# First stage of a routed-attention kernel: low words as unsigned integers on ScalarE, a written order of vector work, deeper loads, later stores

## The chip, the cores and the metric

The kernel runs on one core of a Trainium2 chip. The metric is the device time of one execution in microseconds (us). The engines are TensorE (PE, matrix products; PEld is its weight load), VectorE (DVE), ScalarE (ACT), GpSimd (POOL) and SyncE (SP), which here only issues DMA transfers.

## The reference

Three steps, each feeding the next. Attention packs K and V of 8 batches, 8 heads, 576 tokens into 32 rows per head and reads them back with the queries; a dense layer follows, `g = h - tanh(h)`, and then a layer of 8 experts of which each token takes two.

```
p_packed = sm_attn(p, k, v)                 # 32 rows per head
out      = sm_attn(q, p_packed, p_packed)   # 576 rows per head
x = transpose(out).reshape(4608, 512)
h = x @ w_in;  x = (h - tanh(h)) @ w_out    # 512 -> 2048 -> 512
...                                         # two experts of eight for each row
out[mask] += top2_w[mask, k, None] * (relu(x[mask] @ w1[e]) @ w2[e])
```

The weights `w_in` and `w_out` come as 8-byte floats, which the kernel brings to 4 bytes itself.

## The kernel before

There are three stages, one after the other in the program: `phase_a`, `phase_b`, `PhaseC`.

**First stage, `phase_a`.** It has 16 units, one for each batch and half of the heads. A unit loads keys and packing rows (`load_k`, tile `kT`, 608 KB) and values (`load_v`, 576 KB). Then `s1` multiplies (PE, tile `s`), `max1` takes the negated row maximum (DVE, lines 180 and 181, tile `nm`), `exp1` the exponentials (ACT, line 187, tile `a`), `t1` transposes them (PE, line 199, tile `tp`), `a1t` copies them out (ACT, `a1T`), `pv` multiplies by the values (PE, line 211), `recip1` (DVE, 192 and 193) and `pz2` (DVE, 216, tile `Pz`) scale and mask, `pt` transposes (PE, 221), `pt_out` copies out (ACT, `PT`) and `pt_store` stores 64 KB to memory.

Between the units' steps lies the widening of 28 pieces of `w_in` and `w_out`, class `Widen`. A piece is 128x512 8-byte numbers (512 KB, tile `cvr`). Its high words go through ACT (`act1`, line 69), then DVE (lines 73, 75, 76), its low words through DVE (line 78, which makes a float of the bits) and ACT (`act2`, line 84, which waits for line 78); DVE then makes the scale (line 80) and joins both (`dve2`, lines 88 and 91). That is seven DVE and two ACT instructions for each piece. Four more pieces go the same way in the second stage (tiles `cvc_b`, `cvf_b`, raw tile `wor`).

The loop runs 18 steps. A step handles two pieces (14 steps have them), the scores of unit n and the rest of unit n-1. The string `ORDER` says in what sequence the steps are written, and PE, SP and ACT keep that sequence; DVE's instructions are put in order by the scheduler. SP issues loads and stores from one queue in that order: a store that waits for `PT` holds the loads behind it. Keys and values have two buffers each, raw pieces three.

In steps 3 to 8 the loop also runs the first query chunk (`Queries`, lines 278 to 335): its scores `sq`, two transpositions, a maximum, exponentials, a sum, a transposition to tile `a`. The tiles `q` (the queries as loaded) and `a` share one buffer. `Queries.split` makes `a2h` (ACT) and `a2l` (DVE, line 101) of `a`; it is written at the start of the second stage.

**Second stage, `phase_b`.** It first multiplies `u` (PE, 442, psum tiles of two buffers), splits it into `uh` (ACT, 447) and `ul` (DVE, 451), and then runs 256 steps of `g1` (PE, `h`), `gate` (ACT tanh `t`, DVE `g`), `gsplit` (`gh`, `gl`) and `g2` (PE, `acc`). Around them, a table of steps (`at`) places the widening of the last four pieces, the splits `woh`/`wol`, and constants (`consts_b`) in its first steps. Here PE, ACT, DVE and SP keep the written order.

Of the kernel before, what the change touches and what calls it, by code (L numbers as in the profile page):

```python
# [50 lines left out]
class Widen:  # L51
# [15 lines left out]
    def act1(self):  # L67
        self.c = self.tile("c", F32)
        self.K.nc.scalar.activation(self.c, self.hi.bitcast(F32), AF.Abs)

    def dve(self):
# [6 lines left out]
        V.tensor_scalar(self.f, self.lo, 9, 0x3F800000, op0=ALU.logical_shift_right, op1=ALU.bitwise_or)  # L78
# [25 lines left out]
ORDER = """t1 a1t s1 p0 lk p1 max1 p2 p4 pl r4 rec pv pz2 p3 exp1 pt r0 pto pts qs r1 lv qm qx r2 r3 qa rl""".split()  # L104
ENG = {mybir.EngineType.PE, mybir.EngineType.SP, mybir.EngineType.Activation}
NWA = 12


def phase_a(K, kT, v, w_in, w_out, wide_in, wide_out):
# [4 lines left out]
    with ExitStack() as ctx:  # L114
        right = ctx.enter_context(ExitStack())
        ld = right.enter_context(tc.tile_pool(name="a_ld", bufs=2, side="right"))
# [17 lines left out]
        def cv_load(i):  # L134
            if i < 16:
# [6 lines left out]
            if wide:  # L142
                raw = cv.tile([P, 2 * CW], I32, tag="cv_raw", name=f"cvr_{i}")
# [88 lines left out]
        def on(n, *fs):  # L232
            if 0 <= n < 16:
# [13 lines left out]
        cv_load(1)
        load_v(0)
        for n in range(18):
            c0, c1 = 2 * n, 2 * n + 1  # L250
            ops = {
                "s1": lambda: on(n, s1), "max1": lambda: on(n, max1), "exp1": lambda: on(n, exp1),
                "t1": lambda: on(n - 1, t1), "a1t": lambda: on(n - 1, a1t), "rec": lambda: on(n - 1, recip1),
                "pv": lambda: on(n - 1, pv), "pz2": lambda: on(n - 1, pz2), "pt": lambda: on(n - 1, pt),
                "pto": lambda: on(n - 1, pt_out),
                "qs": lambda: n in (3, 5) and [f() for f in qs[n]], "qm": lambda: n == 6 and [f() for f in qs[n]],
                "qx": lambda: n == 7 and [f() for f in qs[n]], "qa": lambda: n == 8 and [f() for f in qs[n]],
                "pts": lambda: on(n - 1, pt_store),
                "lk": lambda: on(n + 2, load_k), "lv": lambda: on(n + 1, load_v),
                "p4": lambda: None, "r4": lambda: None,  # L260
                "p0": lambda: cv_step(c0, 0), "p1": lambda: cv_step(c0, 1), "p2": lambda: cv_step(c0, 2), "p3": lambda: cv_step(c0, 3),
                "r0": lambda: cv_step(c1, 0), "r1": lambda: cv_step(c1, 1), "r2": lambda: cv_step(c1, 2), "r3": lambda: cv_step(c1, 3),
                "pl": lambda: cv_load(c0 + 2) if c0 + 2 < 16 + NWA else None, "rl": lambda: cv_load(c1 + 2) if c1 + 2 < 16 + NWA else None,
# [88 lines left out]
def consts_b(K, pp, pq, zero, w_gate, w_noise):  # L352
# [39 lines left out]
def phase_b(K, stack, wo_stack, qT, w1, w2, w_out, wide_out, noise, w_gate, w_noise, out):  # L392
# [9 lines left out]
    Q = K.Q = Queries(K, qT, qp, wq, None)  # L402
    yield
# [14 lines left out]
    with ExitStack() as ctx:  # L418
# [306 lines left out]
        def wo_step(i, p):
# [627 lines left out]
```

## Time and profile before

| | us |
|---|---|
| median of 3 runs | 1736.63 |
| range of the runs | 1735.43 to 1743.21 |
| the profiled execution, its own time | 1745.8 |
| its span | 1743.7 |
| PE busy in the span | 1627.6 (93%) |
| DVE busy | 1140.2 (65%) |
| ACT busy | 860.2 (49%) |
| first stage, from the first maximum to the first `ul` | about 7.0 to 151.5 |

The span is what the profiler saw of one execution. A share of busy time is a mean over stages: PE is busy for nearly all of the span after 210 us, and for about two thirds of the first stage. How a stage is bounded is read from which wait ends last in it. The granted clock (PEclk) is a share of 2.4 GHz; 0.50 is the lower level, 1.2 GHz.

### The profile page before, as it was taken

To read this page: it belongs to the slowest core of one execution; us is meant where nothing else is said; L and a number is where in the kernel's file an instruction comes from. 1 tells how busy PE (TensorE), PEld (TensorE's weight loads), DVE (VectorE), ACT (ScalarE), POOL (GpSimd) and SP (SyncE) were. 2 spreads that over 40 slices of the span, in tenths; PEclk is the share of its full clock that TensorE was granted. 3 is DMA by queue.
4 is the path that set the end of the run, shared out by engine and by line. 5 is a ranking of instruction groups with operands and counts; after the bars stand their busy time and mean duration, and the time that the engine had idled before them with its cause. 6 is when DMAs were issued, how large, how long until landed. Compare 5 with 4: busy or idle time off the path is not lost.

```text
span 1743.7 us, 29334 instructions
## 1 busy us (share of the span) xinstructions
PE 1627.6 (93%) x10031; PEld 1383.9 (79%) x10031; DVE 1140.2 (65%) x2910; ACT 860.2 (49%) x1812; POOL 565.5 (32%) x559
## 2 busy tenths in 40 slices
PE   5667999999999999999876899999999999999996
PEld 3435889898989899989765688888888888888885
DVE  7886867676767676766454466666666666666652
ACT  3444555555555555443252355555555555555552
POOL 0000200121212121222454555555555554555521
PEclk7677999999999999999898899999999999999998
DMA  8784367586778787732327665523673236722621
GB/s 276 229 274 117 101 217 251 184 263 195 239 234 255 228 253 221 242 118 76 104 48 271 199 208 175 151 49 77 213 237 54 49 80 210 242 49 49 216 57 25
DMA packets 145653, 293.59 MB, mean 168 GB/s; under 512 B 19682, under 2 KB 69130, under 8 KB 140380
## 3 DMA queue, kind: packets, MB, share of 16 engines
q1 hardware_dynamic: 121676, 252.17, 43.2%
q0 software_dynamic: 23824, 39.51, 12.5%
q8 instruction: 80, 1.31, 0.3%
q14 instruction: 73, 0.60, 0.1%
HBM read 687.34 MB, written 107.59 MB: 456 GB/s over the span
## 4 chain that ended last, share of the span: by engine, by line
PE 86%; DVE 7%; ACT 2%; issue 2%; DMA 1%; POOL 1%; DVEq 0%; POOLq 0%; ACTq 0%
PE acc L501 23%; PE ph L1120 22%; PE py L1162 22%; PE h L476 12%; PE u L442 2%; PE s L175 2%; ACT ht L1142 1%; PE tp L199 1%; PE pv L211 1%; PE sq L299 1%; DVE cva L76 1%; PE lg L522 1%; DMA kT<-in_kT_dram 1%; DVE nm L180 1%; DVE cvf L88 0%
## 5 line engine op out<-in xcount | busy, mean ns | idle before, releaser
L1142 ACT ACTIVATE ht<-h 32x256 f32<-32x256 f32 x624 | 259.6, 416 | 267.7 <-DVE h L1122 129.0
L1120 PE MATMUL ph<-w0s,xh 128*128 128x512 f32 x1200 | 377.4, 396 | 15.0 <-issue 7.8
L1162 PE MATMUL py<-w1s,hh 128*128 128x512 f32 x1200 | 373.6, 392 | 6.4 <-issue 6.4
L981 POOL DMA_INDIRECT x<-x1d,gidxm x276 | 265.0, 960 | 315.0 <-DVE xt L991 246.0
L501 PE MATMUL acc<-gh,wol 128*128 128x288 f32 x1024 | 302.8, 296 | 3.0 <-issue 2.6
L501 PE MATMUL acc<-gl,woh 128*128 128x288 f32 x1024 | 302.2, 295 | 2.0 <-issue 2.0
L501 PE MATMUL acc<-gh,woh 128*128 128x288 f32 x1024 | 302.2, 295 | 1.6 <-issue 1.5
L1122 DVE STREAM_TRANSPOSE h<-ph 128x512 f32<-128x512 f32 x150 | 107.3, 716 | 275.1 <-PE ph L1120 231.7
L1120 PEld LDWEIGHTS ph<-w0s,xh 128*128 128x128 f32 x1200 | 228.9, 191 | 63.8 <-issue 8.2
L1162 PEld LDWEIGHTS py<-w1s,hh 128*128 128x128 f32 x1200 | 227.6, 190 | 56.1 <-issue 8.7
L1162 PE MATMUL py<-w1s,hl 128*128 128x512 f32 x600 | 235.8, 393 | 8.1 <-DVE hl L1151 6.4
L1120 PE MATMUL ph<-w0s,xl 128*128 128x512 f32 x600 | 236.6, 394 | 0.3 <-issue 0.3
L656 POOL DMA_INDIRECT table<-d,qi x96 | 97.0, 1011 | 352.0 <-DVE g L485 270.5
L501 PEld LDWEIGHTS acc<-gh,wol 128*128 128x128 f32 x1024 | 193.1, 189 | 4.0 <-issue 3.5
L501 PEld LDWEIGHTS acc<-gl,woh 128*128 128x128 f32 x1024 | 193.2, 189 | 2.6 <-issue 2.6
L501 PEld LDWEIGHTS acc<-gh,woh 128*128 128x128 f32 x1024 | 193.5, 189 | 2.1 <-issue 2.1
L1140 DVE TENSOR_SCALAR ht<-h 32x256 f32<-32x256 f32 x576 | 177.9, 309 | 10.6
L483 ACT ACTIVATE t<-h 128x288 f32<-128x288 f32 x256 | 104.2, 407 | 151.6 <-PE h L476 133.5
L476 PE MATMUL h<-a2h,uh 128*128 128x288 f32 x512 | 159.4, 311 | 2.8 <-DVE g L485 1.8
L97 ACT ACTIVATE gh<-g 128x288 fp32r<-128x288 f32 x256 | 113.2, 442 | 92.2 <-DVE g L485 90.2
L485 DVE TENSOR_TENSOR g<-h,t 128x288 f32<-128x288 f32 x256 | 115.8, 452 | 60.8 <-ACT t L483 56.3
L476 PE MATMUL h<-a2h,ul 128*128 128x288 f32 x512 | 151.7, 296 | 0.2 <-DVE ul L451 0.2
(230 smaller groups left out, 2394.0 us busy)
## 6 DMA issues: line engine op xcount, KB each, us to landing
w0s<-wsp SPq DMA_DIRECT2D x140, 2048.0 KB
w1s<-wsp SPq DMA_DIRECT2D x140, 2048.0 KB
wsp<-wt SPq DMA_DIRECT2D x128, 512.0 KB
wt<-in_w_dram SPq DMA_DIRECT2D x128, 256.0 KB
kT<-in_kT_dram SPq DMA_DIRECT2D x16, 608.0 KB
out_dram<-zero SPq DMA_DIRECT2D x37, 256.0 KB
v<-in_v_dram SPq DMA_DIRECT2D x16, 576.0 KB
q<-in_qT_dram SPq DMA_DIRECT2D x32, 288.0 KB
```

Of the source, the lines that this page charges most:

```text
L97: nc.scalar.activation(hi, src, AF.Copy)
L476: nc.tensor.matmul(h[:, :TN], u[:, G, fs], x[:, G, :], start=(n == 0), stop=(n == 5))
L483: nc.scalar.activation(t, h[:, :TN], AF.Tanh)
L485: PACE[0] = nc.vector.tensor_tensor(g, h[:, :TN], t, op=ALU.subtract).ins
L501: nc.tensor.matmul(ACC[ch][d][:, :TN], w[:, d * P:(d + 1) * P], x, start=(f == 0 and n == 0), stop=(f == 15 and n == 2))
L656: ins = nc.gpsimd.indirect_dma_start(out=K.table, out_offset=IO(ap=qi[:, i:i + 1], axis=0), in_=d[:, i, :], in_offset=None, oob_is_err=True)
L981: g = K.nc.gpsimd.indirect_dma_start(out=x[:, b, :], out_offset=None, in_=rows, in_offset=IO(ap=gidx[:, c, b:b + 1], axis=0))
L1120: K.nc.tensor.matmul(p, xx[:, d * P:(d + 1) * P], w[:, fc, ws, d, :], start=(n == 0), stop=(n == 11))
L1122: self.last = V.transpose(h[:, 2 * fc:2 * fc + 2].rearrange("p g n -> p (g n)"), p).ins
L1140: V.tensor_scalar(dst, src, 0.0, None, op0=ALU.max)
L1142: K.nc.scalar.activation(dst, src, AF.Relu)
L1162: K.nc.tensor.matmul(p, xx[:, f * P:(f + 1) * P], w[:, f // 4, ws, f % 4, :], start=(n == 0), stop=(n == 23))
```

## The change

In `Widen` the DVE instruction on the low words is gone (line 78): ACT reads the raw low words as unsigned integers and scales them by 2^-52 itself, so it no longer waits for DVE. DVE has six instructions for each piece, and tiles `f` and `t` have two buffers and not three. In `phase_a` DVE joins the engines that keep the written order; `ORDER` is another string; the scores run one unit ahead of the rest; the pieces are spread over 17 steps, one or two in each; raw pieces have eight buffers and are loaded six ahead, keys three and values two units ahead with three buffers each; a unit's store is issued in the step after its own. The first part of `consts_b` (constants, and two small loads of `w_gate` and `w_noise` to tile `wg`) and the zero tile are written ahead of the first stage; only `pre` and what is stored from it stay in the second. Lines of the changed kernel lie a little lower: 73 is 74, 75 is 76, 76 is 77, 88 is 87, 91 is 90, 84 is 83, 180 is 182.

```diff
-            return self.pool.tile([P, self.n], dt, tag=f"cv_{tag}", name=f"cv{tag}_{self.name}", bufs=2 if tag in "ca" else 3)
+            return self.pool.tile([P, self.n], dt, tag=f"cv_{tag}", name=f"cv{tag}_{self.name}", bufs=2)
...
         self.f = self.tile("f", I32)
-        V.tensor_scalar(self.f, self.lo, 9, 0x3F800000, op0=ALU.logical_shift_right, op1=ALU.bitwise_or)
         self.t = self.tile("t", I32)
...
-    def act2(self):
-        u = self.f.bitcast(F32)
-        self.K.nc.scalar.activation(u, u, AF.Copy, scale=2.0 ** -20, bias=-(2.0 ** -20))
+    def act(self):
+        self.K.nc.scalar.activation(self.f.bitcast(F32), self.lo.bitcast(U32), AF.Copy, scale=2.0 ** -52)
...
-ORDER = """t1 a1t s1 p0 lk p1 max1 p2 p4 pl r4 rec pv pz2 p3 exp1 pt r0 pto pts qs r1 lv qm qx r2 r3 qa rl""".split()
-ENG = {mybir.EngineType.PE, mybir.EngineType.SP, mybir.EngineType.Activation}
+ORDER = """lk l0 l1 lv ps max1 exp1 v0 t1 u0 b1 a1t s1 qm w0 v1 u1 pv qx b0 w1 rec pz2 pt qs qa pto""".split()
+ENG = {mybir.EngineType.PE, mybir.EngineType.SP, mybir.EngineType.Activation, mybir.EngineType.DVE}
 NWA = 12
+AHEAD = 6
...
-        ld = right.enter_context(tc.tile_pool(name="a_ld", bufs=2, side="right"))
+        ld = right.enter_context(tc.tile_pool(name="a_ld", bufs=3, side="right"))
...
-                raw = cv.tile([P, 2 * CW], I32, tag="cv_raw", name=f"cvr_{i}")
+                raw = cv.tile([P, 2 * CW], I32, tag="cv_raw", name=f"cvr_{i}", bufs=AHEAD + 2)
...
+        def chunks(n):
+            lo, hi = (min(16 + NWA, (16 + NWA) * k // 17) for k in (n, n + 1))
+            return tuple(lo + i if lo + i < hi else None for i in range(2))
...
+        s1(0)
+        cv_step(0, 0)
+        for n in range(17):
+            c0, c1 = chunks(n)
+            d0, d1 = chunks(n + 1)
...
+                "s1": lambda: on(n + 1, s1), "max1": lambda: on(n, max1), "exp1": lambda: on(n, exp1),
...
+                "pto": lambda: on(n, pt_out), "ps": lambda: on(n - 1, pt_store),
...
+                "lk": lambda: on(n + 3, load_k), "lv": lambda: on(n + 2, load_v),
+                "v0": lambda: cv_step(c0, 1), "u0": lambda: cv_step(c0, 2), "w0": lambda: cv_step(c0, 3),
+                "v1": lambda: cv_step(c1, 1), "u1": lambda: cv_step(c1, 2), "w1": lambda: cv_step(c1, 3),
+                "b0": lambda: cv_step(d0, 0), "b1": lambda: cv_step(c1, 0),
...
+    consts = consts_b(K, wq, zero, w_gate, w_noise)
+    next(consts)
     yield
...
-        consts = consts_b(K, cpre, wq, zero, w_gate, w_noise)
-        at(1, next, consts)
         at(3, next, consts, None)
```

**DVE in a unit of the first stage.** Of before, from the fifth unit's maximum (line 180); `cvf`, `cva`, `cvc` and `cvt` are the tiles of a piece, the number behind a name tells buffers of different pieces apart:

```order
L180 TENSOR_REDUCE nm_457<-s_4_436 128x1
L91 TENSOR_TENSOR WI<-cvf_368,cva_365 128x512
L73 TENSOR_SCALAR cvc_402<-cvc_402 128x512
L78 TENSOR_SCALAR cvf_416<-cvr_340 128x512
L75 TENSOR_SCALAR cva_413<-cvc_402 128x512
L181 TENSOR_SCALAR nm_457<-nm_457 128x1
L76 SCALAR_TENSOR_TENSOR cva_413<-cvr_340,cva_413 128x512
L80 TENSOR_SCALAR cvt_418<-cva_413 128x512
L88 TENSOR_TENSOR cvf_416<-cvf_416,cvt_418 128x512
L78 TENSOR_SCALAR cvf_453<-cvr_376 128x512
L91 TENSOR_TENSOR WI<-cvf_416,cva_413 128x512
L73 TENSOR_SCALAR cvc_445<-cvc_445 128x512
```

Of after, from the same unit's maximum:

```order
L182 TENSOR_REDUCE nm_479<-s_4_421 128x1
L183 TENSOR_SCALAR nm_479<-nm_479 128x1
L74 TENSOR_SCALAR cvc_453<-cvc_453 128x512
L76 TENSOR_SCALAR cva_486<-cvc_453 128x512
L77 SCALAR_TENSOR_TENSOR cva_486<-cvr_184,cva_486 128x512
L80 TENSOR_SCALAR cvt_490<-cva_486 128x512
L87 TENSOR_TENSOR cvf_489<-cvf_489,cvt_490 128x512
L90 TENSOR_TENSOR WI<-cvf_489,cva_486 128x512
L74 TENSOR_SCALAR cvc_500<-cvc_500 128x512
L76 TENSOR_SCALAR cva_516<-cvc_500 128x512
L77 SCALAR_TENSOR_TENSOR cva_516<-cvr_247,cva_516 128x512
L80 TENSOR_SCALAR cvt_520<-cva_516 128x512
```

The small second step of the maximum now follows the first at once, and the instructions of a piece stand one behind the other, each reading what the one ahead of it wrote, where pieces were mixed before.

**SP at the end of the first stage.** The queue of transfers; `q` is the second query chunk, `wor` the first raw pieces of the second stage, `ptd` the stored `PT`. Of before:

```order
L160 DMA kT_1203<-in_kT_dram 128x1216
L287 DMA q_1458<-in_qT_dram 128x2x288
L230 DMA ptd<-PT_1243 128x128
L166 DMA v_1254<-in_v_dram 96x1536
L287 DMA q_1458<-in_qT_dram 128x2x288
L411 DMA wor_1461<-in_w_out_dram 128x1024
L230 DMA ptd<-PT_1302 128x128
L166 DMA v_1305<-in_v_dram 96x1536
L230 DMA ptd<-PT_1350 128x128
L411 DMA wor_1465<-in_w_out_dram 128x1024
```

Of after:

```order
L146 DMA cvr_1166<-in_w_out_dram 128x1024
L168 DMA v_1168<-in_v_dram 96x1536
L232 DMA ptd<-PT_1163 128x128
L232 DMA ptd<-PT_1238 128x128
L232 DMA ptd<-PT_1296 128x128
L232 DMA ptd<-PT_1357 128x128
L300 DMA q_1451<-in_qT_dram 128x2x288 x2
L428 DMA wor_1454<-in_w_out_dram 128x1024
L428 DMA wor_1458<-in_w_out_dram 128x1024
L805 DMA out_dram<-zero 512x1x128
```

The queries and the raw pieces `wor` now stand behind the last four stores.

**DVE at the start of the second stage.** Of before, from the gate of the second step:

```order
L485 TENSOR_TENSOR g_1_1497<-h_1_1488,t_1_1495 128x288
L355 MEMSET tri 96x96
L358 MEMSET ones 96x128
L362 TENSOR_SCALAR ebase<-eio 128x8
L364 TENSOR_SCALAR eio_1508<-eio 128x8
L367 TENSOR_REDUCE fold<-ident 128x16
L369 MEMSET msum 96x8
L371 MEMSET wg 128x128
L376 MEMSET quarter 32x1 x4
L378 MEMSET pre 128x256
L73 TENSOR_SCALAR cvc_b_1463<-cvc_b_1463 128x512
L75 TENSOR_SCALAR cvc_b_1463<-cvc_b_1463 128x512
```

Of after, from the end of the first stage (`a2l` stood between pieces of the first stage before):

```order
L90 TENSOR_TENSOR wof_1165<-cvf_1376,cva_1373 128x512
L100 TENSOR_TENSOR a2l_1421<-a_856,a2h_1420 128x576
L465 TENSOR_TENSOR ul_0_1435<-u_0_0_1424,uh_0_1434 128x512
L465 TENSOR_TENSOR ul_0_1435<-u_0_1_1425,uh_0_1434 128x512
L499 TENSOR_TENSOR g_0_1449<-h_0_1440,t_0_1447 128x288
L100 TENSOR_TENSOR wol_1460<-wof_629,woh 128x512
L100 TENSOR_TENSOR gl_0_1478<-g_0_1449,gh_0_1477 128x288
L499 TENSOR_TENSOR g_1_1490<-h_1_1481,t_1_1488 128x288
L74 TENSOR_SCALAR cvc_b_1456<-cvc_b_1456 128x512
L76 TENSOR_SCALAR cvc_b_1456<-cvc_b_1456 128x512
L77 SCALAR_TENSOR_TENSOR cvc_b_1456<-wor_1454,cvc_b_1456 128x512
L80 TENSOR_SCALAR cvf_b_1495<-cvc_b_1456 128x512
```

The constants no longer stand between the gate and the piece, and `a2l` has moved to the end of the stage.

## Rows read from the trace of the kernel before

**Rows 1.** Stretches; busy us of each engine, granted clock, DMA share, GB/s:

```profile
7.00:151.50 144.50, 94.08 (x768) 57.22 (x768) 117.64 (x285) 62.39 (x123) 2.69 (x2) 0.70 0.78 247
151.50:210.00 58.50, 49.33 (x360) 42.15 (x360) 48.83 (x100) 31.80 (x71) 13.72 (x12) 0.91 0.24 69
```

**Rows 2.** DVE groups, 7 to 140 us; busy us, mean ns, idle before:

```profile
L180 DVE TENSOR_REDUCE nm<-s 128x1 f32<-128x576 f32 x15 | 11.3, 755 | 14.4 <-PE s L175 14.4
```

**Rows 3.** Timeline of DVE: start, us, line, tiles; one piece:

```profile
53.59 0.42 DVE L73 TENSOR_SCALAR cvc<-cvc 128x512 f32<-128x512 f32 x1
54.05 0.43 DVE L75 TENSOR_SCALAR cva<-cvc 128x512 int32<-128x512 int32 x1
54.51 0.69 DVE L76 SCALAR_TENSOR_TENSOR cva<-cvr,cva 128x512 int32<-128x512 int32 x1
55.23 0.43 DVE L80 TENSOR_SCALAR cvt<-cva 128x512 int32<-128x512 int32 x1
55.77 0.69 DVE L88 TENSOR_TENSOR cvf<-cvf,cvt 128x512 f32<-128x512 f32 x1
56.49 0.69 DVE L91 TENSOR_TENSOR WI<-cvf,cva 128x512 f32<-128x512 f32 x1
57.10 0.42 DVE L78 TENSOR_SCALAR cvf<-cvr 128x512 int32<-128x512 int32 x1
57.44 0.42 DVE L73 TENSOR_SCALAR cvc<-cvc 128x512 f32<-128x512 f32 x1
```

**Rows 4.** Timeline of all engines, one unit's chain; idle before and releaser in brackets:

```profile
88.82 0.14 DVE L181 TENSOR_SCALAR nm<-nm 128x1 f32<-128x1 f32 x1
...
89.08 0.74 ACT L187 ACTIVATE a<-s,nm 128x576 f32<-128x576 f32 x1 [2.66 <-DVE nm L181]
...
89.96 1.51 PE L199 MATMUL tp<-ident,a 128*96 128x128 f32 x6 [0.36 <-ACT a L187]
...
91.40 2.07 PE L175 MATMUL s<-kT 64*32 64x288 f32 x16
...
93.41 1.53 PE L211 MATMUL pv<-v,a1T 96*64 96x128 f32 x24
```

**Rows 5.** The same stretch, line 211 alone: busy PE, PEld, clock, DMA:

```profile
7.00:151.50 144.50, 33.79 (x384) 29.13 (x384) 0.70 0.78 247
```

**Rows 6.** Two short stretches around one unit's products, all engines:

```profile
90.00:93.00 3.00, 3.00 (x22) 1.58 (x22) 1.91 (x5) 2.53 (x5) 0.00 (x0) 0.50 0.59 137
94.00:96.50 2.50, 0.94 (x18) 0.69 (x14) 2.50 (x7) 0.63 (x1) 0.00 (x0) 1.00 1.01 326
```

**Rows 7.** Timeline of DVE, end of the first unit:

```profile
15.20 0.35 DVE L216 SCALAR_TENSOR_TENSOR Pz<-pv,rs,mask 128x128 f32<-128x128 f32 x1 [0.41 <-PE pv L211]
```

**Rows 8.** Timeline of all engines, start of the second stage:

```profile
151.49 1.29 DVE L451 TENSOR_TENSOR ul<-u,uh 128x512 fp32r<-128x512 f32 x2 [1.75 <-ACT uh L447]
...
153.57 0.69 ACT L69 ACTIVATE cvc_b<-wor 128x512 f32<-128x512 f32 x1
...
156.50 0.45 DVE L485 TENSOR_TENSOR g<-h,t 128x288 f32<-128x288 f32 x1
...
159.34 0.36 DVE L73 TENSOR_SCALAR cvc_b<-cvc_b 128x512 f32<-128x512 f32 x1
...
161.48 1.28 DVE L451 TENSOR_TENSOR ul<-u,uh 128x512 fp32r<-128x512 f32 x2
...
162.22 2.56 PE L442 MATMUL u<-WI,pt 64*32 64x512 f32 x16 [6.19 <-DVE ul L451]
```

**Rows 9.** Timeline of SP's queue (SPq) and of the load's first reader:

```profile
0.81 0.40 SPq L160 DMA_DIRECT2D kT<-in_kT_dram  x1
...
4.83 2.14 PE L175 MATMUL s<-kT 64*32 64x288 f32 x16 [4.83 <-DMA kT<-in_kT_dram]
...
133.83 0.55 SPq L287 DMA_DIRECT2D q<-in_qT_dram  x1
134.43 0.59 SPq L411 DMA_DIRECT2D wor<-in_w_out_dram  x1
```

More of the change, by code (lines that the diff above doesn't have):

```diff
@@ L34, in _sint @@
     return u - (1 << 32) if u >= (1 << 31) else u
+U32 = mybir.dt.uint32
 EXP_LO = _fbits(896 << 20)
@@ L65, in tile, with abs @@
         return self.pair[:, 1].bitcast(dt)
-    def act1(self):
+    def abs(self):
         self.c = self.tile("c", F32)
@@ L134, in cv_load @@
         def cv_load(i):
+            if i is None or i >= 16 + NWA:
+                return
             if i < 16:
@@ L151, in cv_step @@
                 x = CV[i]
-                (x.act1, x.dve, x.act2, x.dve2)[part]()
+                (x.abs, x.dve, x.act, x.dve2)[part]()
                 if part == 3:
@@ L246, in phase_a @@
         load_k(1)
-        cv_load(1)
         load_v(0)
-        for n in range(18):
-            c0, c1 = 2 * n, 2 * n + 1
+        for i in range(1, 4):
+            cv_load(i)
+        load_v(1)
+        load_k(2)
+        for i in range(4, AHEAD):
+            cv_load(i)
+        s1(0)
[3 more added lines that the diff above has]
+            d0, d1 = chunks(n + 1)
             ops = {
[L252 to L255, printed above, removed]
+                "s1": lambda: on(n + 1, s1), "max1": lambda: on(n, max1), "exp1": lambda: on(n, exp1),
+                "t1": lambda: on(n, t1), "a1t": lambda: on(n, a1t), "rec": lambda: on(n, recip1),
+                "pv": lambda: on(n, pv), "pz2": lambda: on(n, pz2), "pt": lambda: on(n, pt),
+                "pto": lambda: on(n, pt_out), "ps": lambda: on(n - 1, pt_store),
@@ L349, with consts_b @@
 NSURE = 75
-def consts_b(K, pp, pq, zero, w_gate, w_noise):
+def consts_b(K, pp, zero, w_gate, w_noise):
     nc, cp = K.nc, K.cpool
@@ L376, in consts_b @@
         nc.vector.memset(K.quarter[32 * q:32 * q + 32], float(q))
-    pre = pq.tile([P, P, 2], F32, tag="st", name="pre")
+    yield
+    pre = pp.tile([P, P, 2], F32, tag="st", name="pre")
     nc.vector.memset(pre, 0.0)
     nc.gpsimd.iota(pre[:, :, 0], pattern=[[1, P]], base=N, channel_multiplier=0, allow_small_or_imprecise_dtypes=True)
-    yield
     tv = K.table.rearrange("(r l) two -> r (l two)", l=P)
@@ L402, in phase_b @@
     Q = K.Q = Queries(K, qT, qp, wq, None)
+    zero = wq.tile([P, P], F32, name="zero")
+    nc.vector.memset(zero, 0.0)
+    consts = consts_b(K, wq, zero, w_gate, w_noise)
+    next(consts)
     yield
@@ L430, in phase_b @@
         wol = []
-        zero = wp.tile([P, P], F32, name="zero")
-        nc.vector.memset(zero, 0.0)
         ET = mybir.EngineType
@@ L730, in wo_step @@
                 x.w = K.wo_pool.tile([P, DM], F32, tag="wo", name=f"wof{i}")
-            (x.act1, x.dve, x.act2, x.dve2)[p]()
+            (x.abs, x.dve, x.act, x.dve2)[p]()
             K.wof[i] = x.w
```

8 lines of the change are left out of this document (1 added, 7 removed).

## The prediction, made before the changed kernel was run

> **What bounds the kernel now.** I read the busy slices of the page first: PE is near full from 210 us to the end, so a shift in what lies before is passed on, and nothing after it is touched by the change. Then I read the stretches before that. In the first stage, 7.0 to 151.5 us, no engine is full: DVE 117.6 of 144.5 us, PE 94.1, ACT 62.4, the transfers 0.78 [rows 1]. DVE is the nearest to full, and the largest part of its idle time, 14.4 us, is waiting for the scores' product ahead of the maximum [rows 2]. So the stage is a ring in which DVE and PE take turns. Its end for this argument is the first `ul`, at 151.49 [rows 8], since all of the second stage follows from it. I call that moment T. Behind it the chain runs through DVE until about 210 us: PE stands idle 6.19 us for the second pair of `ul` [rows 8], and DVE is busy 48.8 of 58.5 us [rows 1]. The sum is made against the profiled execution, 1745.8 us, which lies 9.2 us above the median of 1736.6; the difference that I find is taken over to the median.
>
> **DVE's work on a piece.** One instruction of seven goes, line 78. Its slot is 0.34 us (57.10 to 57.44) [rows 3], so 28 pieces give up at most 9.5 us. But the written order puts each instruction of a piece right behind the one whose result it reads, and such pairs start 0.46, 0.46, 0.72, 0.54 and 0.72 us apart, while the independent step from 57.10 to 57.44 took 0.34 for the same 0.42 us instruction [rows 3]. The stretch at 53.59 happens to be the new sequence: from line 73 to the end of line 91's slot it is 0.46 + 0.46 + 0.72 + 0.54 + 0.72 + 0.61 = 3.51 us. Two pieces: 7.02. What dropping line 78 saves is thus largely paid back as waits between neighbours; I cost the new order as a whole and not as a difference.
>
> **A unit of the new order.** With 28 pieces in 17 steps, units 1 to 15 hold ten with two pieces and five with one; unit 0 has one, and the step behind the last unit has two.
> A unit with two pieces is DVE's: maximum 0.76 [rows 2] and 0.03 to its second step, 0.1 for that, 7.02, two small steps at 0.18 (0.14 [rows 4] and the gap), 0.27 for `Pz`: 8.5 us. Ten: 85.0.
> A unit with one piece leaves DVE idle, and the ring decides: `Pz` 0.3, maximum 0.79, its second step to the exponentials 0.26 (88.82 to 89.08), to the transposes 0.88, to the scores 1.44, to `pv` 2.01, then `pv` and 0.06 to `Pz` [rows 4]. `pv` took 1.53 there; over the stage sixteen of them took 33.79 us, 2.11 each [rows 5]. That makes 7.3 to 7.85 us. I take 7.5, nearer to the former, because the new order also runs transposes, scores and `pv` without a gap, as in rows 4. Five: 37.5.
> The first unit ends as before, with `Pz` at 15.20, for which DVE waited on `pv` [rows 7]: its one piece (3.5 us) fits in front of that. The loads of `wg` and the constants ahead of it delay its first loads by about 1 us; I take nothing for it, 1.1 us at most.
> The query steps: maximum, sum, and two transpositions (one in halves) are four passes over 576 columns like that of line 180, 0.76 each, 3.0 in all; small steps 0.4; and since the order puts the query scores right ahead of their transposition, DVE waits for that product, between 1 and 2 us as it is shaped like the scores' (2.01 [rows 4]), 1.5. Together 4.9.
> `Pz` of unit 15 is then at 15.2 + 85.0 + 37.5 + 4.9 = 142.6. Behind it stand 0.3, two more pieces (7.0) and `a2l`, a pass like the maximum, 0.76, which no longer runs between pieces: T = 150.7, against 151.5 before: **0.8 us earlier**. Bounds: with `pv` at half speed throughout (3.06, estimated as twice 1.53) the ring is 8.8 us for every unit, and T is 3.0 + 6.5 later, 160.2; with everything on PE at the high clock the one-piece ring is 1.44/2 + 2.01/2 us shorter than 7.3, 5.6, and T is 141.2.
>
> **The loads.** Keys, values and pieces come far ahead, and the store no longer holds them. That takes waits from SP and a few from ACT; on DVE and PE, which make the sum above, I find none to remove but the ring itself. What it costs: thirteen loads are queued in the first microseconds. The stage moves 16 x 1184 KB + 28 x 512 KB, some 34 MB, and about 2 MB of stores and queries; at the mean 247 GB/s [rows 1] that is 146 us, so the loads could become the bound if they got no faster. In the short stretch at 94.0 us they moved 326 GB/s [rows 6], by which it is 110 us. I take no cost; the first rate would add 5.
>
> **A new wait at the start of the second stage.** `a2l` reads the tile that the next queries are loaded into, and it now runs last in the first stage. In the queue those queries, and behind them the raw pieces `wor`, start only then; before, they were issued at 133.83 and 134.43 [rows 9]. From T: two issues at 0.55 to 0.6, then `wor`, which I let land 4.0 us after its issue, as the first load of the program did (issued 0.81, used 4.83 [rows 9]): T + 5.2. ACT's step on it stood at 153.57, T + 2.08 [rows 8], and ACT keeps its order: behind it wait the split of the weights, `uh` and the next gate. From that step to the gate on DVE it is 2.93 us (156.50), and 0.4 to the next start, so DVE begins the piece at T + 8.5. The constants that lay there are gone (156.91 to 159.34, 2.4 us), and of the piece four dependent instructions remain, 0.46 + 0.46 + 0.72 + 0.45 = 2.1: the second `ul` at T + 10.6, where it stood at 161.48, T + 10.0 [rows 8]. **0.6 us later** against T. Had `wor` been in time it would be 2.8 us earlier; if it lands at T + 6.1 (the queries 4.0, then 512 KB at 247 GB/s), 1.5 later.
> Three more pieces in this stage save 0.34 each on DVE; I count two as on the chain, **-0.7** (0 to -1.0). `pre` is filled later than before, and the store from it must land before the query transposition writes the same buffer: 0 to 1 us, **+0.3**.
>
> **Sum.** -0.8 + 0.6 - 0.7 + 0.3 = -0.6: 1745.2 for an execution like the profiled one, 1736.0 for the median.
>
> **The rivals.** (1) *PE's clock stays high*: the granted clock is 0.70 on average here [rows 1]; with longer runs of products it could hold, T is 9.5 us earlier: 1726.5. For it: the clock went from 0.50 to 1.00 within one unit's run [rows 6]. Against: a unit of 8 us still has a gap of about 2.5 us ahead of its transposes. (2) *DVE saves all of line 78*, because the waits between neighbours also lie in the order before: -9.5, about 1726.5. Against: before, half of the neighbours are independent. (3) *The ring at the low clock*, slower: at 90.0 to 93.0 PE was busy all the time at 0.50, and at 94.0 it stood at 1.00 [rows 6], so `pv` ran at the higher level only after transposes and scores in one run. Should the transposes not help to raise it, `pv` is slow in every unit, T is 160.2 and the time 1745.5; it decides as soon as `pv` takes over 2.2 us in two-piece units as well, where the ring then passes 8.5.
> The Trainium skill ("TensorE: Matmul & The Clock Gate", section "Part 4: PE-mode transpose") has a rule for this: transposes do not count as busy PE in the same way, and the higher clock does not engage for them. By that rule (3) would hold. The trace speaks against it in the one run of rows 6, where transposes were 1.44 us of the 3.45 us between 89.96 and 93.41 [rows 4] and the clock rose all the same.
> (4) *The loads bound*: +5, 1740.5.
>
> **How the numbers follow.** Chances: the forecast 0.66 (1731 to 1740), (1) 0.07, (2) 0.09, (3) 0.08, (4) 0.10. A measurement of this kernel can tell about 0.5%, 8.7 us. (1) and (2) lie on that bound, and give faster by more than it 0.13; (3) and the upper tail of (4) give slower 0.08; within it 0.79. The range takes in the bounds of `wor`, `pre` and the loads and the near side of both ends, and the spread of the runs before (1735.4 to 1743.2): 1727 to 1745. What I choose: 1736.0.
>
> **What would show it.** Right: units of the first stage some 8.5 and 7.5 us apart in the profile of after, DVE with almost no idle time in the two-piece ones and waiting for `pv` at `Pz` in the others; the first `ul` between 148 and 154 us; ACT idle some 3 us ahead of its first step on `wor`, released by a transfer; no constants between the gate and the piece. Wrong: units of under 7 us, or a first `ul` before 145 or after 157; DVE waiting for a transfer in the first stage; ACT not waiting for `wor`, which would make it 3 us faster.

## The result: slower by 0.9%, in two places ahead of the long stretch

The changed kernel took 1754.0 us (median of 5 runs, 1751.5 to 1755.2), the kernel before 1735.4 on the same chip: ratio 1.0088, 95% interval 1.0062 to 1.0113. I had forecast 1736.0, within 1727 to 1745, and given slower by over 0.5% a chance of 0.08. The measured time lies outside the range.

First the stretches of the changed kernel, beside [rows 1] (columns as there):

```profile
7.00:163.60 156.60, 92.16 (x773) 55.67 (x769) 119.53 (x259) 64.36 (x124) 2.93 (x2) 0.76 0.77 221
163.60:222.00 58.40, 47.60 (x334) 39.79 (x335) 44.33 (x81) 28.28 (x63) 12.36 (x10) 0.86 0.31 93
```

DVE is busy 119.5 us with 259 instructions, where it was 117.6 with 285: the removal of line 78 was paid back between neighbours, as the sum had it. (Without the new order, in x6_u32 below, DVE is busy 112.7 us up to its first `ul`.) But the stage is 12 us longer. The timeline of DVE gives the ends, start in us first, beside [rows 8]; of after:

```profile
155.72 0.35 DVE L218 SCALAR_TENSOR_TENSOR Pz<-pv,rs,mask 128x128 f32<-128x128 f32 x1
...
163.66 1.28 DVE L465 TENSOR_TENSOR ul<-u,uh 128x512 fp32r<-128x512 f32 x2
178.49 1.28 DVE L465 TENSOR_TENSOR ul<-u,uh 128x512 fp32r<-128x512 f32 x2
184.71 1.22 DVE L465 TENSOR_TENSOR ul<-u,uh 128x512 fp32r<-128x512 f32 x2
198.90 1.28 DVE L465 TENSOR_TENSOR ul<-u,uh 128x512 fp32r<-128x512 f32 x2
```

The fourth `ul` of before:

```profile
182.74 1.28 DVE L451 TENSOR_TENSOR ul<-u,uh 128x512 fp32r<-128x512 f32 x2
```

The first `ul` stands at 163.66 (151.49 before), the fourth at 198.90 (182.74 before). So 12.2 us are lost in the first stage, 4.0 more up to the fourth `ul`, 16.2 in all; the medians differ by 18.5, the ratio says 10.8 to 19.6.

**Where the first stage went.** The starts of `Pz`, unit by unit, against the terms of my sum:

| | forecast us | measured us | lost |
|---|---|---|---|
| `Pz` of unit 0 | 15.2 | 17.0 | 1.8 |
| unit 1 (two pieces) | 8.5 | 10.9 | 2.4 |
| unit 3 (two pieces) | 8.5 | 14.7 | 6.2 |
| units 6, 7, 9 with the query steps | 30.4 | 31.6 | 1.2 |
| units 2, 5, 8, 11, 14 (one piece) | 37.5 | 38.6 | 1.1 |
| units 4, 10, 12, 13, 15 (two pieces) | 42.5 | 42.9 | 0.4 |
| from there to the first `ul` | 8.1 | 7.9 | -0.2 |

The first three rows hold 10.4 of the 13.0 us, and in all three an engine waits for a transfer. The timelines of SP's queue, PE and ACT around them (idle time before and its releaser in brackets):

```profile
26.66 0.34 SPq L232 DMA_DIRECT2D ptd<-PT  x1
```
```profile
11.69 2.15 PE L177 MATMUL s<-kT 64*32 64x288 f32 x16 [0.97 <-DMA kT<-in_kT_dram]
...
23.80 2.14 PE L177 MATMUL s<-kT 64*32 64x288 f32 x16 [3.16 <-DMA kT<-in_kT_dram]
...
44.41 1.52 PE L201 MATMUL tp<-ident,a 128*96 128x128 f32 x6 [8.10 <-ACT a L189]
```
```profile
15.07 0.67 ACT L70 ACTIVATE cvc<-cvr 128x512 f32<-128x512 f32 x1 [3.51 <-DMA cvr<-in_w_in_dram]
...
43.36 0.28 ACT L228 ACTIVATE PT<-pt 128x128 f32<-128x128 f32 x1 [10.40 <-DMA ptd<-PT]
...
69.46 0.28 ACT L228 ACTIVATE PT<-pt 128x128 f32<-128x128 f32 x1 [5.50 <-DMA ptd<-PT]
```

In unit 0 PE waits for the second keys (11.69), which were issued 1.3 us later than before, behind the loads of `wg`. In unit 1 PE waits for the third keys (23.80), and `pv` and `Pz` follow them. ACT's wait for a piece at 15.07 held nothing: it was done at 15.74, and DVE came to that piece at 18.12. In unit 3, at 43.36, it is a store: `PT` has two buffers, so the copy of unit 2 waits for the store of unit 0, which was issued at 26.66 behind all the loads queued by then and let go 16.7 us later, for 64 KB. ACT keeps its order, so the exponentials of the next unit stand behind that copy, and PE's transposes behind them (8.10 us). The Trainium skill ("DMA: Bandwidth & Descriptors", section "Queues, rings and completion order") says that SP has one ring on each of the 16 DMA engines and that descriptors are consumed in ring order; the 16.7 us agree with a small store that waits its turn. From the rows: nine loads, 5.05 MB, were issued between the third keys and that store; at 288 GB/s (the row from 7 to 60 us further down) they would end 17.5 us after 23.80, at 41.3, an estimate that fits the 43.36. The second wait for a store, 5.50 us at 69.46, cost nothing: unit 6 took 11.8 us with it, and as long in x1_pt4 without it.

**The start of the second stage.** From ACT's timeline:

```profile
172.28 0.66 ACT L70 ACTIVATE cvc_b<-wor 128x512 f32<-128x512 f32 x1 [6.05 <-DMA wor<-in_w_out_dram]
```

and from SP's queue:

```profile
163.77 1.21 SPq L300 DMA_DIRECT2D q<-in_qT_dram  x2
165.04 1.07 SPq L428 DMA_DIRECT2D wor<-in_w_out_dram  x2
```

The wait that I forecast is there, and longer: `wor` was read 7.2 us after its issue, at T + 8.6; the second `ul` came at T + 14.8.

### The profile page after: what moved, and what is told of

It reads as the page before. It is cut to its first block, busy times and chain, and to the rows that moved or that the text cites. A ratio compares the mean times of both kernels' runs of the same rounds, so it can differ in the third digit from the quotient of the medians.

```text
span 1753.5 us, 29382 instructions
## 1 busy us (share of the span) xinstructions
PE 1622.9 (93%) x10031; PEld 1380.3 (79%) x10031; DVE 1139.7 (65%) x2878; ACT 860.5 (49%) x1812; POOL 564.5 (32%) x559
## 4 chain that ended last, share of the span: by engine, by line
PE 82%; DVE 7%; DMA 4%; ACT 3%; issue 2%; another core or an unknown queue 1%; SPq 0%; POOL 0%; DVEq 0%; POOLq 0%; ACTq 0%
PE ph L1132 22%; PE py L1174 22%; PE acc L515 21%; PE h L490 12%; PE u L456 2%; DMA v<-in_v_dram 2%; ACT ht L1154 1%; DMA cvr<-in_w_in_dram 1%; DVE cvf L87 1%; DMA ptd<-PT 1%; PE sq L312 1%; PE lg L536 1%; ACT a L189 0%; DVE g L499 0%
## 5 line engine op out<-in xcount | busy, mean ns | idle before, releaser
L490 PE MATMUL h<-a2l,uh 128*128 128x288 f32 x512 | 152.3, 297 | 3.7 <-DVE a2l L100 3.7
```

What stands on the lines that cost most here:

```text
L490: nc.tensor.matmul(h[:, :TN], u[:, G, fs], x[:, G, :], start=(n == 0), stop=(n == 5))
```

## The experiments

All in one table. "First" and "fourth" are the starts of the first and fourth `ul` in the profile, "before us" is the kernel before on the same chip in the same rounds; from chip to chip it differs by up to 9 us, so rows are compared by their ratios.

| run | first | fourth | median us | before us | ratio (95%) |
|---|---|---|---|---|---|
| the changed kernel | 163.7 | 198.9 | 1754.0 | 1735.4 | 1.0088 (1.0062 to 1.0113) |
| x1_pt4 | 159.1 | 194.9 | 1746.1 | 1733.8 | 1.0071 (1.0049 to 1.0093) |
| x2_ahead2 | 163.5 | 198.3 | 1749.0 | 1733.8 | 1.0097 (1.0078 to 1.0116) |
| x3_split | 161.0 | 190.4 | 1744.4 | 1733.8 | 1.0071 (1.0053 to 1.0089) |
| x4_start | 157.7 | 187.0 | 1738.1 | 1732.6 | 1.0031 (1.0018 to 1.0044) |
| x5_mix | 154.9 | 183.3 | 1730.0 | 1732.6 | 0.9986 (0.9968 to 1.0005) |
| x7_auto | 159.3 | 189.5 | 1741.4 | 1732.6 | 1.0052 (1.0034 to 1.0070) |
| x12_ring | 151.0 | 181.6 | 1730.7 | 1733.6 | 0.9986 (0.9970 to 1.0003) |
| before, again (x0_before) | 151.5 | 182.7 | 1734.2 | 1733.8 | one run |
| x6_u32 | 141.4 | 171.4 | 1724.5 | 1732.6 | 0.9953 (0.9936 to 0.9970) |
| x8_dveorder | 151.0 | 182.7 | 1738.7 | 1741.4 | 0.9980 (0.9962 to 0.9999) |
| x9_loads | 149.0 | 179.3 | 1736.8 | 1741.4 | 0.9973 (0.9960 to 0.9985) |
| x11_consts | 146.8 | 176.7 | 1735.4 | 1741.4 | 0.9962 (0.9946 to 0.9977) |
| x10_spread | 130.0 | 161.8 | 1723.8 | 1741.4 | 0.9898 (0.9878 to 0.9918) |
| x13_spread16 | 143.3 | 173.8 | 1724.8 | 1733.6 | 0.9944 (0.9927 to 0.9960) |
| x14_ahead3 | 142.9 | 178.5 | 1731.4 | 1733.6 | 0.9981 (0.9970 to 0.9991) |

**The profile of before, once more** (no edit):

> The kernel before, unchanged, for the profile of another execution. The profiled execution of before took 1745.8 us where the median of the runs was 1736.6. If the 9 us lie in the first stage, the first ul of this one stands near 142.5 us and not at 151.5; if they lie behind it, the first ul stands at 151 to 152 again and the rest of the span is some 9 us shorter than 1592.2 us. A third way: this execution also takes about 1745 and tells nothing.

The first `ul` came at 151.47 and the fourth at 182.73, as in the first profile to 0.02 us; the span was 1732.1 us, 11.6 shorter. So what lifted the first profile above its median lies in the long stretch behind, and the first stage of this kernel comes out alike. One pair of executions does not show how far it varies in kernels whose transfers are late; unit 0 in the next runs gives a measure of that.

**Late stores.** In the changed kernel:

```diff
-            t["PT"] = sm.tile([P, P], F32, tag="PT", name=f"PT{n}")
+            t["PT"] = sm.tile([P, P], F32, tag="PT", name=f"PT{n}", bufs=4)
```

> The changed kernel with four buffers instead of two for tile PT, nothing else. In the profile of after ACT stood 10.40 us (unit 2) and 5.50 us (unit 5) at the copy to PT, released by a store of an older PT, and unit 3 took 14.7 us where the others with two pieces take 8.6. Theory 'late stores': the stores land late behind the loads that are queued far ahead, and two buffers are too few; then both waits are gone, unit 3 takes 8.5 to 10 us, the first ul stands 5 to 8 us earlier than 163.7, and the time is 5 to 8 us below the changed kernel's 1754.0. Rival 'the loads are the bound there': unit 3 then waits for keys, values or a piece instead, the first ul moves by under 2 us, and the time is within 2 us of 1754.

Both waits for a store are gone and unit 3 takes 8.6 us. The first `ul` is 4.6 us earlier, just under the 5 that I had set, because units 0 to 2 took 1.4 us longer than in the changed kernel. Late stores are shown as the cause of unit 3 by the profile; the ratios, 1.0071 and 1.0088, are too close for their intervals to tell apart.

**A shallower queue of pieces.** With it the first loads hold two pieces and not six:

```diff
-AHEAD = 6
+AHEAD = 2
```

> The changed kernel with raw pieces loaded two ahead (four buffers), keys and values as far ahead as in after. Theory 'queue too deep': in the first microseconds four loads of 512 KB less stand ahead of the third keys, and stores find a shorter queue; units 0 and 1, which took 17.0 us to the first Pz and 10.9 us, come to 15.2 to 16 and about 8.6, unit 3 loses most of its 6 us, the first ul stands 6 to 10 us earlier than 163.7, the time is 6 to 10 us below 1754.0. Rival 'the depth pays': ACT waits for pieces in each unit with two, by 1 us or more, and the first ul is later than 163.7.

Neither: the waits for stores are gone (unit 3 takes 8.6), but ACT now waits 31.1 us for raw pieces, since the third piece is queued behind the fourth keys (unit 1 takes 13.4), and the first `ul` stays. ACT's group of the kernel with two ahead (count, busy us, mean ns, idle before and releaser):

```profile
L70 ACT ACTIVATE cvc<-cvr 128x512 f32<-128x512 f32 x28 | 18.6, 666 | 31.1 <-DMA cvr<-in_w_in_dram 31.1
```

With this order of work depth moves the wait; it does not remove it.

**Late wor.** In the changed kernel the split of the first queries is taken a step after `a`, in the first stage:

```diff
-              8: (lambda: Q.out(0),)}
+              8: (lambda: Q.out(0),), 9: (lambda: Q.split(0),)}
...
-        Q.split(0)
         for k in range(4):
```

> The changed kernel with a2h and a2l of the first queries taken a step after tile a in the first stage, as they lay in the kernel before, so that the next queries and the raw pieces wor are issued before the stage ends. Theory 'late wor' (the new wait that I forecast): the first ul stays at 163 to 165, ACT's first step on wor comes before T + 3 instead of at T + 8.6, the second ul at T + 7 to T + 9 instead of T + 14.8, and the time is 5 to 7 us below 1754.0. Rival: the second ul is then held by its products or the gate and stands at T + 10 as in before (4 to 5 us), or what is won there is lost again at the third and fourth ul (0 to 2 us).

The second `ul` stands at T + 9.2 instead of T + 14.8, the fourth at T + 29.3 instead of T + 35.2: 5.9 us, as this theory has it, though its second `ul` stands just above the T + 9 that I had set. ACT no longer waits for `wor` (T is 161.04 here):

```profile
163.45 0.67 ACT L70 ACTIVATE cvc_b<-wor 128x512 f32<-128x512 f32 x1
```

The first `ul` came 2.6 us earlier as well, most of it in unit 0 (`Pz` at 15.2, not 17.0), though the first loads are the same; why they landed sooner I don't know. So the 1.8 us of unit 0 in the table above do not come in every execution: `Pz` stood at 17.2 in x1_pt4, with the same first loads too.

**The first loads in order of need**, with the two edits above:

```diff
-        for i in range(1, 4):
+        for i in range(1, 3):
             cv_load(i)
-        load_v(1)
         load_k(2)
-        for i in range(4, AHEAD):
+        load_v(1)
+        for i in range(3, AHEAD):
```

> The changed kernel with three edits together: four buffers for PT, a2h and a2l taken in the first stage, and the first loads in the order of their need (third keys ahead of the second values and of the fourth piece, which stood ahead of them). One theory is that three waits on transfers (late stores, late wor, late keys at the start) are the whole of what the changed kernel loses against the sum: then unit 1 takes 8.5 to 9.5 us instead of 10.4 to 11.6, the first ul comes at 152 to 157, the second at T + 9, and the time is within 4 us of the kernel before (1734). Rival: the transfers are the bound of the first units as a whole, at some 280 GB/s; then what the third keys win the pieces lose, unit 1 stays at 10 to 11 us, the first ul is 157 to 160 and the time 1738 to 1742.

Unit 1 takes 8.6 us, as the theory has it; the first `ul` (157.7) and the median lie in the rival's ranges: unit 2 now takes 9.9, its `pv` waiting for values. At the fourth `ul` 11.9 of the 16.2 us are won back, so transfers account for most of what the changed kernel loses against the kernel before, and still it is no faster than that. T is 7.0 us above my sum, 4.5 of it in the units with one piece, which take 8.4 us in the mean and not 7.5. So the next question is where the gain of line 78 went.

**Line 78 alone**, in the kernel before:

```diff
-        V.tensor_scalar(self.f, self.lo, 9, 0x3F800000, op0=ALU.logical_shift_right, op1=ALU.bitwise_or)
...
-        self.K.nc.scalar.activation(u, u, AF.Copy, scale=2.0 ** -20, bias=-(2.0 ** -20))
+        self.K.nc.scalar.activation(self.f.bitcast(F32), self.lo.bitcast(U32), AF.Copy, scale=2.0 ** -52)
```

> The kernel before with the low words as unsigned integers on ScalarE and nothing else: line 78's 28 instructions (and 4 in the second stage) are gone from DVE, which the scheduler orders as it did. My sum says that the removal is worth at most 9.5 us in the first stage where neighbours stay independent, and almost nothing where they become dependent. Theory 'DVE bound': first ul at 142 to 146, time 6 to 10 us below the kernel before. Rival 'ring of PE and DVE': the units of before wait for the product of the scores ahead of the maximum in any case, the first ul stands at 149 to 152 and the time is within 3 us.

```profile
141.40 1.29 DVE L450 TENSOR_TENSOR ul<-u,uh 128x512 fp32r<-128x512 f32 x2 [2.90 <-ACT uh L446]
```

10.1 us earlier, and 0.47% faster, more than the 9.5 us that I had put as the most that line 78 could give. The other parts of the change cost the first stage 22 us from there. The next runs add them one at a time to this kernel.

**The written order of DVE.** Once added to this kernel (`ENG` with DVE), once taken from x4_start:

> The kernel x6_u32 (before, with line 78 gone; 1724.5 us, first ul at 141.4) with DVE added to the engines that keep the written order in the first stage, ORDER as in before. One part of the change alone. Theory 'waits between neighbours': the instructions of a piece then stand one behind the other, a unit with two pieces rises from 8.4 to 9 us or more, the first ul is at 146 to 152, the time 1729 to 1735. Rival, after x7_auto (where giving the order back to the scheduler won nothing): the order of DVE is worth under 2 us either way, first ul at 139.5 to 143.5, time 1722 to 1727.

> As x4_start, with DVE left to the scheduler in the first stage as in the kernel before; ORDER, depths and spread as in after. It tells what the written order of DVE is worth. If the order mixes the pieces, neighbours are independent and units with two pieces fall from 8.6 to 7.5 to 8 us, the first ul is 4 to 10 us earlier than in x4_start. Rival: Pz and the maximum then wait behind pieces' instructions, PE waits for them, and the first ul is the same or up to 5 us later than in x4_start.

Added, the first `ul` goes to 151.0. But 4.7 us of these 9.6 come at the start (`Pz` of unit 0 at 19.0, not 14.3): in before's `ORDER` a piece stands ahead of the first maximum, and DVE waits for that piece's load. Units 4 to 8, around the query steps, take 8.2 us more together, and the rest is 3.4 us shorter. The waits between neighbours are there, since DVE is busy 117.6 us and not 112.7 with the same 258 instructions; but units 9 to 12, with two pieces, take 8.4 to 8.7 us in both. Taken from x4_start, nothing is won (159.3 against 157.7). So it is not in the length of a plain unit that these waits cost here. A direct look at them:

**Two pieces in turn**, and 28 pieces over 16 steps, on x4_start:

```diff
-ORDER = """lk l0 l1 lv ps max1 exp1 v0 t1 u0 b1 a1t s1 qm w0 v1 u1 pv qx b0 w1 rec pz2 pt qs qa pto""".split()
+ORDER = """lk l0 l1 lv ps max1 exp1 v t1 u0 a1t s1 qm u1 w pv qx b0 b1 rec pz2 pt qs qa pto""".split()
...
-            lo, hi = (min(16 + NWA, (16 + NWA) * k // 17) for k in (n, n + 1))
+            lo, hi = (min(16 + NWA, (16 + NWA) * k // 16) for k in (n, n + 1))
```

> As x4_start, and the two pieces of a unit go through DVE in turn (the same step of both, then the next), so that no instruction reads what the one ahead of it wrote, and the 28 pieces are spread over 16 steps instead of 17, so that none lies behind the last unit. Theory 'waits between neighbours' (3.51 us for a piece in a row, 2.85 without them): a unit with two pieces falls from 8.6 to the ring's 7.3 to 7.7 us, nothing stands ahead of ul but a2l, the first ul comes at 138 to 145, and the time is 8 to 16 us below the kernel before. Rival: DVE has a fixed cost for each instruction whatever it reads, two pieces in turn take 7.0 us as before, the units stay at 8.5 and only the tail's 7 us are won, less 0.9 us for each unit that now has two pieces instead of one: first ul at 147 to 152, time within 6 us of the kernel before.

DVE's timeline of one unit (the pairs are grouped):

```profile
103.72 0.42 DVE L74 TENSOR_SCALAR cvc<-cvc 128x512 f32<-128x512 f32 x1
104.05 0.76 DVE L77 TENSOR_SCALAR cva<-cvc 128x512 int32<-128x512 int32 x2
104.72 1.29 DVE L79 SCALAR_TENSOR_TENSOR cva<-cvr,cva 128x512 int32<-128x512 int32 x2
105.93 0.75 DVE L83 TENSOR_SCALAR cvt<-cva 128x512 int32<-128x512 int32 x2
...
109.27 0.15 DVE L206 TENSOR_SCALAR rs<-rs 128x1 f32<-128x1 f32 x1
```

Two pieces took 5.55 us where in a row they take 7.0: the waits between neighbours are real, 0.7 us for a piece. Yet the first `ul` came only 2.8 us earlier than in x4_start, outside the ranges of both theories. 4.3 us of it are the tail, where no piece is left, so units 0 to 15 took 1.5 us more together; those with two pieces took 7.2 to 11.2 without query steps: something else holds them. In x4_start and x5_mix PE stands idle 26.4 and 25.9 us ahead of the transposes, for the exponentials; in before it was 5.4:

```profile
L211 PE MATMUL pv<-v,a1T 96*64 96x128 f32 x384 | 33.8, 343 | 13.8 <-ACT a1T L204 13.8
...
L199 PE MATMUL tp<-ident,a 128*96 128x128 f32 x96 | 22.9, 408 | 5.4 <-ACT a L187 5.4
```

**The loads and the constants**, each alone on x6_u32:

> The kernel x6_u32 with the loads and stores of the changed kernel and nothing else: raw pieces eight buffers and six ahead, keys and values three buffers, issued first in a step, the first loads in the order of the changed kernel, the store a step later. Theory 'the deep queue costs': the third keys, pieces and stores are late in the first units as in the changed kernel, ACT waits 5 us or more for a store of PT, the first ul is at 146 to 152 instead of 141.4, the time 1729 to 1735. Rival: in the order of work of before these transfers have slack, first ul within 2 us of 141.4.

> The kernel x6_u32 with the constants and the zero tile written ahead of the first stage, as in the changed kernel, and nothing else. By my sum the constants held DVE for 2.4 us ahead of the piece at the start of the second stage: the second ul comes at T + 7.0 to T + 8.0 instead of T + 9.8, the first ul stays within 1 us of 141.4 (two small loads stand ahead of the second keys), and the time is 1 to 3 us below x6_u32's 1724.5. Rival: the second ul is held by ACT's work ahead of it and the time stays within 1 us.

The deep loads and late stores of the changed kernel (with its two buffers for tiles `f` and `t`, which this run takes over too) put the first `ul` 7.6 us later; ACT waits seven times for a store of `PT`, 42.8 us in all, of which the two longest are:

```profile
44.20 0.28 ACT L226 ACTIVATE PT<-pt 128x128 f32<-128x128 f32 x1 [9.67 <-DMA ptd<-PT]
...
65.94 0.28 ACT L226 ACTIVATE PT<-pt 128x128 f32<-128x128 f32 x1 [9.87 <-DMA ptd<-PT]
```

The constants ahead of the stage, which I had counted as nothing there (1.1 us at most), put it 5.4 us later, against the 1 us of either theory. They save 1.0 us behind it (second `ul` at T + 8.8, not T + 9.8) where I had 2.4. What happens shows in the transfers of the first 10 us, x11_consts first, x6_u32 second:

```profile
DMA packets 1668, 2.57 MB, mean 257 GB/s; under 512 B 1118, under 2 KB 1118, under 8 KB 1668
```
```profile
DMA packets 666, 2.84 MB, mean 284 GB/s; under 512 B 65, under 2 KB 65, under 8 KB 666
```

The two loads of `wg`, 16 KB each, are a thousand small packets. ACT's first piece, which it needs ahead of the first exponentials, came at 8.26 and not at 6.15; the second piece and the first values were then late too, and `Pz` of unit 0 came 3.7 us later. The constants' own instructions on DVE lay in the wait for that piece; no run takes them and the two loads apart.

**The spread of the pieces**, on x6_u32:

```diff
-            c0, c1 = 2 * n, 2 * n + 1
+            lo, hi = (min(16 + NWA, (16 + NWA) * k // 17) for k in (n, n + 1))
+            c0, c1 = (lo + i if lo + i < hi else 99 for i in range(2))
```

> The kernel x6_u32 with the pieces spread over 17 steps, one or two in each, as in the changed kernel. In x6_u32 fourteen units have two pieces at 8.5 us each and the last two have none and take 5.5 and 3.9. Theory 'the spread loses the short units': units with one piece are held by the ring and do not fall to the mean of the two, and two pieces lie near or behind the last Pz; first ul at 145 to 150, time 1728 to 1734. Rival: units with one piece take some 7 us, the sum is the same, first ul within 2 us of 141.4.

Both theories were wrong: the first `ul` came at 130.0, and this kernel beats both the kernel before and the changed one (ratio 0.9898). Its units take 7.2 us in the mean where the changed kernel's take 9.2.

**The ring.** What is left is the scores one unit ahead, with the next maximum behind `Pz`. On x4_start:

```diff
-ORDER = """lk l0 l1 lv ps max1 exp1 v0 t1 u0 b1 a1t s1 qm w0 v1 u1 pv qx b0 w1 rec pz2 pt qs qa pto""".split()
+ORDER = """lk l0 l1 lv ps v0 t1 u0 b1 a1t s1 qm w0 v1 u1 pv max1 exp1 qx b0 w1 rec pz2 pt qs qa pto""".split()
...
-                "s1": lambda: on(n + 1, s1), "max1": lambda: on(n, max1), "exp1": lambda: on(n, exp1),
+                "s1": lambda: on(n + 1, s1), "max1": lambda: on(n + 1, max1), "exp1": lambda: on(n + 1, exp1),
```

> x4_start (first ul at 157.7) with one move in the written order: a unit's maximum and exponentials are taken right behind its scores, one step earlier, ahead of the unit's before it Pz, and not behind that Pz. Theory 'pv lies in the ring': in the changed kernel the next maximum stands behind Pz on DVE, Pz waits for pv, so PE waits for the exponentials ahead of the transposes (26.4 us in x4_start, 32.5 in after, 5.4 in before); without that, units with one piece fall from 8.4 to 5 to 6.5 us, those with two stay at 8.5, where DVE is full, the wait ahead of the transposes is under 8 us, the first ul comes at 140 to 147, the time 11 to 17 us below x4_start's ratio of 1.0031. Rival: the units with one piece are held by the transfers or by PE at the low clock, they stay over 7.5 us, and the first ul moves by under 5 us.

PE's groups, x4_start first, x12_ring second (busy us, mean ns, idle before and releasers):

```profile
L213 PE MATMUL pv<-v,a1T 96*64 96x128 f32 x384 | 36.7, 364 | 3.2 <-DMA v<-in_v_dram 2.0 <-ACT a1T L206 1.0
...
L201 PE MATMUL tp<-ident,a 128*96 128x128 f32 x96 | 22.4, 399 | 26.4 <-ACT a L189 26.4
```
```profile
L213 PE MATMUL pv<-v,a1T 96*64 96x128 f32 x384 | 35.2, 352 | 23.5 <-DMA v<-in_v_dram 19.4 <-ACT cvc L70 2.6 <-ACT a1T L206 1.5
...
L201 PE MATMUL tp<-ident,a 128*96 128x128 f32 x96 | 20.9, 381 | 2.1 <-ACT a L189 2.1
```

The wait ahead of the transposes falls from 26.4 to 2.1 us, as the theory has it, and three of the five units with one piece take 5.9 to 6.6 us. DVE's wait for `pv` ahead of `Pz`, 20.4 us in x4_start, falls to 13.0. The first `ul` gains 6.7 us and not 11 to 17, and PE now waits 19.4 us for values: by these rows the transfers take back a part of what the ring gives, which no further run tests.

**Can x10_spread be bettered?**

> x10_spread (the kernel before, line 78 gone, pieces over 17 steps; ratio 0.9898, first ul at 130.0) with the pieces over 16 steps, so that none is left for the step behind the last unit. In x10_spread 6.6 us lie between the last Pz and the first ul. Theory 'the tail': 3 us of it go, units rise by 0.5 us in the mean of three more with two pieces, first ul at 127 to 130, ratio 0.988 to 0.990. Rival: what the tail gives the units take, first ul at 130 to 133, ratio 0.990 to 0.992.

> x10_spread with raw pieces three ahead instead of two (five buffers instead of three) and four buffers for PT. In x10_spread ACT waits 19.3 us for raw pieces in the first stage, and the transfers are busy for 0.91 of it. Theory 'a little depth helps': half of that wait goes, first ul at 124 to 128, ratio 0.986 to 0.988. Rival 'the transfers are full': the bytes set the end, the wait moves to keys and values, first ul at 129 to 132, ratio as in x10_spread.

No: both lose 13 us of the first stage. With three pieces ahead ACT's wait for raw pieces falls from 19.3 to 1.6 us, and DVE's wait for the scores rises from 10.7 to 26.1. Here DVE is ordered by the scheduler, and the traces show another order after each edit; that x10_spread is faster than x6_u32 is measured, that the spread as such is the cause is not shown, since one step less undoes it.

## Why the prediction was wrong, point by point

**What held.** A unit with two pieces took 8.58 us wherever no transfer disturbed it (forecast 8.5), and DVE was full in it: in the timeline two pieces lie from 98.09 to 105.10, 7.01 us (forecast 7.02). Units with one piece took 7.3 to 8.6, mean 7.7 (7.5), DVE waiting 2.3 to 3.6 us for `pv`. The query steps were 1.2 us longer than counted, the tail 0.2 shorter. The stretch from the second to the fourth `ul` shrank by 0.85 us (forecast, with `pre`, 0.4).

**The step that failed: the loads.** "on DVE and PE, which make the sum above, I find none to remove but the ring itself", then "I take no cost", and for the first unit "I take nothing for it". I asked what rate the stage needs, and found it met. What decides is what stands ahead in the queue. The large loads up to the third keys are 5.14 MB; at the 247 GB/s of [rows 1] that is 20.8 us, from the first issue at 0.81 [rows 9] thus 21.6 at the earliest; PE got them at 23.80. I had all of these numbers. The sum is a lower bound only: in the 23.0 us from 0.80 on the transfers moved 6.6 MB (285 GB/s), so a part of what stood behind had moved as well. And a store issued behind such a queue is as late: 16.7 us, with two buffers of `PT`. Of the 13.0 us between my T and the measured one 10.4 lie in the three places above. DVE itself never waited for a transfer; it waited for PE and ACT, which did. My rival (4), the loads as the bound, had the right resource and a price of 5, but by the rate: after 60 us, the transfers were busy for 0.64 of the time (the second row below), and no unit was lengthened by one.

```profile
7.00:60.00 53.00, 27.36 (x239) 16.50 (x235) 34.41 (x79) 19.14 (x37) 0.00 (x0) 0.85 1.02 288
60.00:163.60 103.60, 64.81 (x534) 39.17 (x534) 85.12 (x182) 45.22 (x88) 2.93 (x2) 0.71 0.64 186
```

These are stretches of the changed kernel: the transfers are full at 288 GB/s while the units wait for them, and idle for a third of the rest.

**The second one: wor.** The mechanism was right and the term too small: read at T + 8.6, where I took T + 5.2 and, as the bound, T + 6.1. I let it land 4.0 us after its issue like the first load of the program [rows 9], which had no load ahead of it; here two loads of queries lie ahead and a second `wor` beside it, and it took 7.2. The term was +0.6 and measured +4.8 at the second `ul`. "Had `wor` been in time it would be 2.8 us earlier" was too much as well: with `wor` in time (x3_split) the second `ul` stood at T + 9.2, 0.8 earlier than before, and the constants alone saved 1.0 where I had counted 2.4.

**The rivals.** (1) fell: the granted clock rose from 0.70 to 0.76 only, and all `pv` together took as long as before, 34.2 us:

```profile
L213 PE MATMUL pv<-v,a1T 96*64 96x128 f32 x384 | 34.2, 346 | 1.7 <-ACT a1T L206 1.0 <-DMA v<-in_v_dram 0.7
```

(2), "DVE saves all of line 78", fell for this kernel, but holds by itself: alone it gives 10.1 us. (3) fell: `pv` was no slower than before; whether transposes help to raise the clock no run isolates. What I had not asked is what the new order does to the ring. I worked out its length rightly, maximum to `Pz` with `pv` inside it, and did not compare it with before, where the next scores, maximum and exponentials run beside `pv`: [rows 4] show the scores of the next unit ahead of `pv`, and the last two units there, without pieces, took 6.3 and 3.9 us. With `pv` in the ring, no unit of the changed kernel took less than 7.3 us; in a unit with two pieces DVE's own 8.5 us hide that. From x6_u32 to x4_start the first `ul` moves by 16.3 us, and taking `pv` out of the ring gives 6.7 of them back: a part of line 78's gain went there. The other 9.6 us are not taken apart. In before's order the deep loads cost 7.6 us and the early constants 5.4, but nothing was tested that adds them up in the new order.

**The median.** I took the difference over from the profiled execution; that was sound, for its excess lay behind the part that changed.

## What to carry to other kernels

Price a deeper prefetch by position: add up the bytes that stand in the queue ahead of the transfer that is needed first, stores too, and compare the landing, which this puts at the earliest, with the time of its reader; a rate that suffices on average says nothing of that. When an engine's work shrinks, draw the ring of dependences in the new order and in the old, and compare their lengths before counting the saving. Try a removal alone before it is bundled with a new order: alone it was worth 0.5% here, and the bundle cost 0.9%.

## What the runs showed of the chip

Two loads of 16 KB in a thousand packets of under 512 B, written ahead of a load of 512 KB, delayed that load's reader by 2.1 us (8.26 against 6.15, x11_consts), of which 1.2 are its later issue (2.51 against 1.27). And a 64 KB store behind queued loads of half a megabyte each took 16.7 us from its issue until the copy that waited for its buffer could start.
